# Attention's four PSUM banks: two tiles of two banks instead of one tile with views over any two, and a new order

## The chip, the cores and the metric

The kernel runs on one core of a Trainium2 chip, as one launch. The metric is the time of the launch on the device in microseconds (us); lower is better. A core has five engines, each with an instruction queue of its own that it works through in order: TensorE (PE; its weight loads are shown apart as PEld), VectorE (DVE), ScalarE (ACT), GpSimd (POOL) and SyncE (SP, which here issues the DMAs). Results of TensorE land in PSUM, which has eight banks of 512 fp32 per partition.

## The reference

Chunked attention with eight memory keys in front of each window, and behind it a gated feed-forward (fp32 in and out; the three FFN weights arrive as float64):

```python
# attention: batch 4, 8 heads, 768 steps, head size 64, chunks of 32
k_ctx = k[:, :, max(0, c0 - 16) : min(S, c0 + 32 + 8)]
k_full = concatenate([mem_k, k_ctx]);  v_full = concatenate([mem_v, v_ctx])
scores = scale * q_c @ k_full.T
a = exp(scores - max(scores));  a = a / (sum(a) + 1e-9)
x[:, :, c0 : c0 + 32] = a @ v_full
# FFN: 512 -> 1024 -> 512
h = maximum(x @ w_in, 0)
conv = sum over k of conv_w[k] * shifted h          # 3 taps along the sequence
out = (h * sigmoid(conv)) @ w_out
```

## The kernel before

**Work.** Attention is cut into 32 steps (batch, half of the sequence, pair of heads) and these into 18 groups: groups 0 to 3 hold one step each, groups 4 to 17 two (m is the number of steps). One group is a chain over four engines. On PE the scores (L382, 48 matmul records a step); on DVE the row maximum (L391); then either a subtraction on DVE and one exp on ACT (L396, L400), or six exps a step straight from PSUM on ACT, with the maximum as bias (L416); clearing of the edge; on DVE the row sum and its reciprocal (L433, L437); the normalisation on DVE or POOL (L440); the turning of the result, on PE (the turn, L452, followed by a copy out of PSUM on ACT, L455) or by way of DVE and a DMA (L462 to L477); on PE the product with the values (L496, 48 records a step); and from its result a rounded part on ACT (the high part, L510) and what is left on DVE (the low part, L513). High and low part are what the FFN reads.

The FFN's matmuls are in three passes (high by high, high by low, low by high): ffn_in (L528, 768 matmuls of 384 columns), the relu that empties its PSUM bank (L538), the gate (L549 to L578 on DVE, ACT and POOL) and ffn_out (L590, 600 matmuls, most of 512 columns). The float64 weights are turned into a high and a low fp32 part on ACT, DVE and POOL (L273 to L352), beside the attention of the first three batches.

**PSUM.** Four banks belong to the FFN (four tiles f). The other four are one tile, `banks`; the pool named s hands out bank numbers 0 to 3. Scores and values take two numbers each, a turn one or two (as many as the group has steps), and `view` makes the access: banks a to z in steps of z - a, so 0 and 1, or 0 and 2, or 1 and 3.

**Order.** Every operation is put down with the function that issues it; `Plan.run` then issues them in the order of the table ORDER, 1301 numbers. Nothing is rearranged behind it: on each engine the instructions stand as ORDER has them, and what waits for what across the engines is drawn from the tiles that they read and write. A tile is given its buffer when its first operation in ORDER is issued, and the buffer goes back behind its last. Strings such as TAP, MULT, LO, NORM hold a letter for each group or FFN column block that says which engine does a step.

Of the kernel before, what the change touches and what calls it, by code (L numbers as in the profile page):

```python
# [21 lines left out]
NG = NC // 4  # L22
# [9 lines left out]
W_IN, W_OUT, W_CONV = "CCCCMRmM", "MCMMMCCM", "r"  # L32
TAP = "AAVAAAAAAAAAAAAAAAVAAAVAVVVVAVAV"
MULT = "VVGGGGGVVVVVVGGGGGVGVVVVGVVVVVVG"
LO = "VVVVVGVVVVVVVVVGGGGVGVGGVVGVVVGV"
SOFT = "AAVAVVVCVVCVVAVVVC"
NORM = "GGVGGVGGVVVVGVVGVG"
CLEAR = "GAGGGAGGAVVGGVAGVG"
KEEP = "NKNNNNNNNNNNKNKKKKNNKKKNNKKKNNNN"
# [146 lines left out]
def act(n, psum=False, ptr=0):  # L186
    return ((192 if psum else 238) + n) / 1.2 + 93 * ptr
# [3 lines left out]
def attention_then_gated_ffn(  # L191
# [44 lines left out]
    slots("top", 4, [P, 4 * NG])  # L236
    slots("z", 4, [P, 4 * NG])

    banks = psum.tile([P, 4, 512], F32, name="banks")
    plan.pool("s", list(range(4)))  # L240

    def view(x, n):
# [471 lines left out]
```

## Time and profile before

| | |
|---|---|
| median of 3 runs | 379.67 us (379.25 to 383.1) |
| the profiled execution | 381.81 us, of it 380.0 us span |
| PE busy | 339.1 us (89%) |
| DVE, ACT, POOL busy | 233.8, 190.3, 73.2 us |
| granted TensorE clock, mean | 0.972 of full speed |

The span is the time from the first instruction to the last in the profiled execution; the 1.8 us around it are launch and end. PE has far the most to do, and in the table of stages of 20 us it is busy without a break from 60 to 80, 120 to 140 and, but for 0.92 us, from 200 to 360 us. Rows with [idle before <-releaser] tell how long the engine had stood idle before them, and whose instruction ended the wait; "issue" means that it waited for nothing that the profile shows.

### The profile page before, as it was taken

What the parts mean: (1) busy time and instruction counts of PE and PEld (TensorE: products, weight loads), DVE (VectorE), ACT (ScalarE), POOL (GpSimd) and SP (SyncE); (2) the same over time, 40 slices, a digit from 0 to 9 for tenths busy, and PEclk for the clock granted to TensorE, in tenths of its full rate; (3) what the DMA queues carried; (4) which work ended last, traced back from release to release, by engine and by line L of the source; (5) the groups of instructions that cost most, each with busy time, mean ns of one, the idle gap of its engine ahead of it and who ended that gap; (6) DMA issues with size and microseconds to landing.
All of it is one profiled execution on the core that took longest, in us unless ns stands there. A gap on an engine that the chain in (4) does not pass through costs nothing.

```text
span 380.0 us, 10189 instructions
## 1 busy us (share of the span) xinstructions
PE 339.1 (89%) x4500; PEld 303.1 (80%) x4500; DVE 233.8 (62%) x325; ACT 190.3 (50%) x347; POOL 73.2 (19%) x69
## 2 busy tenths in 40 slices
PE   1378779997988989797999999999999999999996
PEld 0257679996878979796899887789988998888886
DVE  5864767997678978965887968571011558950000
ACT  4624517976583866773546573843243335541011
POOL 0232413023141000251021001511117002121000
PEclk9999989999898998996999999999999999999999
DMA  8992773998350442402321440224000100002022
GB/s 280 403 397 92 285 259 116 298 345 340 103 180 6 139 154 73 117 0 86 116 83 47 155 144 32 101 96 140 2 2 0 55 29 28 2 28 83 29 83 83
DMA packets 24363, 47.60 MB, mean 125 GB/s; under 512 B 2176, under 2 KB 11136, under 8 KB 24320
## 3 DMA queue, kind: packets, MB, share of 16 engines
q1 hardware_dynamic: 24320, 46.96, 35.9%
q8 instruction: 35, 0.57, 0.6%
q14 instruction: 8, 0.07, 0.1%
HBM read 38.30 MB, written 8.65 MB: 124 GB/s over the span
## 4 chain that ended last, share of the span: by engine, by line
PE 82%; DVE 8%; ACT 5%; issue 4%; DMA 1%; DVEq 0%; ACTq 0%
PE f L590 35%; PE f L528 33%; PE banks L496 8%; PE banks L382 5%; ACT e L416 2%; PE banks L452 2%; DVE u L513 1%; DVE e L396 1%; DVE top L391 1%; ACT u L455 1%; DMA w<-in_w_in_dram 1%; ACT u L510 1%; DVE z L433 1%; DVE w_top L283 1%; DVE w L309 1%
## 5 line engine op out<-in xcount | busy, mean ns | idle before, releaser
L528 PE MATMUL f<-u,w_in_hi 128*128 128x384 f32 x512 | 146.1, 352 | 0.0
L590 PE MATMUL f<-w_out_hi,u 128*128 128x512 f32 (+1 forms) x400 | 127.5, 389 | 0.0
L528 PEld LDWEIGHTS f<-u,w_in_hi 128*128 128x128 f32 x512 | 97.5, 196 | 2.2
L528 PE MATMUL f<-u,w_in_lo 128*128 128x384 f32 x256 | 88.8, 347 | 0.0
L590 PEld LDWEIGHTS f<-w_out_hi,u 128*128 128x128 f32 x400 | 74.6, 189 | 15.5
L590 PE MATMUL f<-w_out_lo,u 128*128 128x512 f32 (+1 forms) x200 | 77.5, 388 | 0.0
L558 DVE SCALAR_TENSOR_TENSOR u<-u,cw,u 128x767 f32<-128x767 f32 x64 | 64.3, 1013 | 3.5 <-ACT u L549 2.6
L538 ACT ACTIVATE u<-f 128x384 f32<-128x384 f32 x64 | 31.2, 493 | 47.5 <-PE f L528 43.0
L528 PEld LDWEIGHTS f<-u,w_in_lo 128*128 128x128 f32 x256 | 50.2, 196 | 1.2
L513 DVE TENSOR_TENSOR u<-banks,u 128x768 fp32r<-128x768 f32 (+1 forms) x18 | 15.5, 867 | 49.4 <-ACT u L510 28.5
L590 PEld LDWEIGHTS f<-w_out_lo,u 128*128 128x128 f32 x200 | 37.8, 189 | 7.0
L572 POOL TENSOR_TENSOR u<-u,u 128x768 f32<-128x768 f32 x13 | 25.6, 1973 | 74.6 <-ACT u L571 74.6
L601 ACT COPY w_top<-f 128x512 f32<-128x512 f32 (+1 forms) x25 | 14.2, 568 | 50.7 <-PE f L590 50.6
L496 PEld LDWEIGHTS banks<-u,u 64*64 64x64 f32 x1296 | 25.2, 162 | 10.7 <-ACT u L455 3.4
L496 PE MATMUL banks<-u,u 64*64 64x32 f32 x1296 | 26.9, 242 | 7.3 <-ACT u L455 2.3
L575 ACT CAST u<-u 128x768 fp32r<-128x768 f32 x32 | 26.4, 836 | 13.4 <-DVE u L567 5.5
L562 ACT ACTIVATE u<-u 128x768 f32<-128x768 f32 x32 | 26.5, 844 | 9.9 <-DVE u L558 9.9
L578 POOL TENSOR_TENSOR u<-u,u 128x768 fp32r<-128x768 f32 x10 | 19.0, 1904 | 56.2 <-ACT u L575 35.4
L382 PE MATMUL banks<-k,u 64*32 64x64 f32 x1344 | 17.5, 236 | 9.3 <-issue 7.8
L578 DVE TENSOR_TENSOR u<-u,u 128x768 fp32r<-128x768 f32 x22 | 21.9, 1008 | 6.1 <-ACT u L575 6.1
L510 ACT CAST u<-banks 128x768 fp32r<-128x768 f32 (+1 forms) x18 | 13.1, 733 | 24.5 <-PE banks L496 11.5
L382 PEld LDWEIGHTS banks<-k,u 64*32 64x32 f32 x1344 | 15.0, 110 | 12.8 <-issue 9.4
(57 smaller groups left out, 304.3 us busy)
## 6 DMA issues: line engine op xcount, KB each, us to landing
u<-in_v_dram SPq DMA_DIRECT2D x27, 384.0 KB, 8.3
k<-in_k_dram SPq DMA_DIRECT2D x14, 528.0 KB, 5.8
out_dram<-w_top SPq DMA_DIRECT2D x23, 256.0 KB, 2.1
u<-in_q_dram SPq DMA_DIRECT2D x14, 384.0 KB, 7.8
w<-in_w_in_dram SPq DMA_DIRECT2D x8, 512.0 KB, 6.1
w<-in_w_out_dram SPq DMA_DIRECT2D x8, 512.0 KB, 3.9
t_dram<-w SPq DMA_DIRECT2D x6, 384.0 KB, 4.1
u<-t_dram SPq DMA_DIRECT2D x12, 192.0 KB, 3.3
```

The costliest lines, as they stand in the source:

```text
L382: nc.tensor.matmul(s_of[j * CH : (j + 1) * CH, u, to : to + KW], lhsT=q_[r, c, h], rhs=k_t.t[r, o : o + KW], start=True, stop=True,)
L496: nc.tensor.matmul(a_of[h * D : (h + 1) * D, u, to : to + CH], lhsT=v_c[r, c, h], rhs=a_d.t[r, o : o + CH], start=True, stop=True,)
L510: plan.op("A", act(m * TW, True), lambda: A.copy(out=apart(part[0]()), in_=a_()), (*a,), (hi,))
L513: lambda: V.tensor_tensor(out=apart(part[1]()), in0=a_(), in1=apart(part[0]()).bitcast(F32), op=ALU.subtract),
L528: nc.tensor.matmul(f.t[:, :TW], lhsT=w_in_p[c][:, fc, cc], rhs=x(a), start=(cc == 0 and i == 0), stop=(cc == NCC - 1 and i == 2),)
L538: "A", act(TW, True), lambda: A.activation(h.t[:, hf * TW : (hf + 1) * TW], f.t[:, :TW], AF.Relu, scale=0.5), (f,), ((h, hf),)
L558: lambda j=j, to=to, at=at: V.scalar_tensor_tensor(out=c.t[:, to], in0=h.t[:, at], scalar=w[j], in1=c.t[:, to], op0=ALU.mult, op1=ALU.add) ...
L562: plan.op("A", act(S), lambda: A.activation(c.t, c.t, AF.Tanh), (c,), (c,), table="exp")
L572: plan.op("G", 2.42 * S, lambda: G.tensor_tensor(out=y.t, in0=c.t, in1=h.t, op=ALU.mult), (c, h), (y,), shared=True)
L575: plan.op("A", act(S), lambda: A.copy(out=g_hi.t, in_=y.t), (y,), (g[0],))
L578: lambda: (V if lo == "V" else G).tensor_tensor(out=g_lo.t, in0=y.t, in1=g_hi.t.bitcast(F32), op=ALU.subtract),
L590: nc.tensor.matmul(ps.t[:, :n], lhsT=gs[b, fc][a].t[:, tt * P : (tt + 1) * P], rhs=w_out_p[c][:, fc, o : o + n], start=(fc == 0 and i == 0 ...
```

## The change

The tile `banks` goes. The pool s now holds two PSUM tiles of two banks each, and scores, turns and values each take one of them whole, the one-bank turns of groups 0 to 3 too. From there ORDER was searched anew, and the strings with it: it has 1302 numbers now, since one more of the gate's products goes to POOL, which takes one more ACT instruction (L571). Counted over the strings, 12 instead of 9 of the 32 first taps are on DVE, 18 instead of 19 of the gate's products, 21 instead of 22 of the low parts of g, 8 instead of 9 normalisations. The number of matmuls is the same.

```diff
-TAP = "AAVAAAAAAAAAAAAAAAVAAAVAVVVVAVAV"
-MULT = "VVGGGGGVVVVVVGGGGGVGVVVVGVVVVVVG"
+TAP = "VAVAAAAAAAAAAAAAAAVVAVAVVVVVAVAV"
+MULT = "VVGGGGGVVVVVVVGGVVVVGGVVGVGGVVGG"
...
 ORDER = [
-    326, 13, 12, 337, 29, 28, 60, 45, 327, 332, 44, 333, 61, 328, 348, 335, 15, 329, 330, 359, 16, 338, 343, 14, 17, 339,
+    326, 13, 12, 337, 29, 28, 60, 44, 327, 332, 45, 333, 348, 328, 61, 335, 15, 329, 330, 14, 338, 343, 16, 77, 17, 339, 18,
...
-    banks = psum.tile([P, 4, 512], F32, name="banks")
-    plan.pool("s", list(range(4)))
-
-    def view(x, n):
-        a, z = min(y.t for y in x), max(y.t for y in x)
-        return banks[:, a : z + 1 : max(1, z - a), :n]
-
+    slots("s", 2, [P, 2, 512], pool=psum)
     slots("f", 4, [P, 512], pool=psum)
...
-        s, e, top, z = [Tile("s"), Tile("s")], Tile("e"), Tile("top"), Tile("z")
+        s, e, top, z = Tile("s"), Tile("e"), Tile("top"), Tile("z")
...
-            s_of = view(s, mg * KW)
+            s_of = s.t
...
-        plan.op("PE", 522 * m, scores, (q_d, k_t), (*s,), mode="t32", late=250)
-        s_ = lambda: view(s, mg * KW).rearrange("p u (g k) -> p g u k", k=KW)
+        plan.op("PE", 522 * m, scores, (q_d, k_t), (s,), mode="t32", late=250)
+        s_ = lambda: s.t[:, :, : mg * KW].rearrange("p u (g k) -> p g u k", k=KW)
...
-        a, a_d = [Tile("s"), Tile("s")], Tile("u")
+        a, a_d = Tile("s"), Tile("u")
         if TURN[n] == "P":
-            t = [Tile("s") for _ in range(m)]
+            t = Tile("s")
...
-            plan.op("PE", 245 * m, turn, (e,), (*t,), mode="whole", late=250)
-            plan.op("A", act(m * TW, True), lambda: A.copy(out=steps(a_d.t[:, : m * TW]), in_=view(t, TW)), (*t,), (a_d,))
+            plan.op("PE", 245 * m, turn, (e,), (t,), mode="whole", late=250)
+            plan.op("A", act(m * TW, True), lambda: A.copy(out=steps(a_d.t[:, : m * TW]), in_=t.t[:, :m, :TW]), (t,), (a_d,))
```

On PE, at the start of the program, these are the scores of groups 0 to 3 and the turn and values of group 0. A name in brackets is an engine's counter that the instruction waits for (DVE_49, Activation_49, Pool_49, or a DMA queue's); u_ and k_ are buffers of q and k. Before:

```order
L382 MATMUL banks<-u_115,u_117 32x64 [waits DMAHW2_49,DMAHW1_49]
L382 MATMUL banks<-u_115,u_117 32x64 x23
L382 MATMUL banks<-u_120,u_122 32x64 [waits DMAHW4_49,DMAHW5_49,DVE_49,Activation_49]
L382 MATMUL banks<-u_120,u_122 32x64 x23
L382 MATMUL banks<-u_126,u_130 32x64 [waits DMAHW7_49,DMAHW0_49,DVE_49]
L382 MATMUL banks<-u_126,u_130 32x64 x23
L382 MATMUL banks<-u_133,u_124 32x64 [waits DMAHW1_49,DMAHW6_49,DVE_49,Activation_49]
L382 MATMUL banks<-u_133,u_124 32x64 x23
L452 MATMUL banks<-ident,e_70 128x128 [waits DVE_49,Pool_49]
```

The same place in the changed kernel:

```order
L375 MATMUL s_98<-u_116,u_118 32x64 [waits DMAHW2_49,DMAHW1_49]
L375 MATMUL s_98<-u_116,u_118 32x64 x23
L375 MATMUL s_99<-u_121,u_123 32x64 [waits DMAHW5_49,DMAHW4_49]
L375 MATMUL s_99<-u_121,u_123 32x64 x23
L375 MATMUL s_98<-u_131,u_127 32x64 [waits DMAHW0_49,DMAHW7_49,DVE_49,Activation_49]
L375 MATMUL s_98<-u_131,u_127 32x64 x23
L375 MATMUL s_99<-u_136,u_125 32x64 [waits DMAHW2_49,DMAHW6_49,DVE_49,Activation_49]
L375 MATMUL s_99<-u_136,u_125 32x64 x23
L444 MATMUL s_98<-ident,e_70 128x128 [waits DVE_49,Pool_49]
```

The instructions stand in the same row; the second scores, which write the other two banks, waited for DVE and ACT and now wait for their data alone.

On ACT, behind the turns of groups 12 and 13: u_2391 and u_2456 (u_2396 and u_2457 in the changed kernel) are the copies of the two turns, L510 (L501) the high parts of their values. Before:

```order
L455 COPY u_2391<-banks 128x768 [waits PE_49,Pool_49]
...
L455 COPY u_2456<-banks 128x768 [waits PE_49]
...
L510 CAST u_2515<-banks 128x2x2x192 [waits DMAHW7_49,PE_49]
...
L510 CAST u_2529<-banks 128x2x2x192 [waits DVE_49]
```

And now:

```order
L447 COPY u_2396<-s_99 128x768 [waits PE_49]
...
L447 COPY u_2457<-s_98 128x768 [waits PE_49]
...
L501 CAST u_2516<-s_99 128x2x2x192 [waits PE_49]
...
L501 CAST u_2523<-s_98 128x2x2x192 [waits DVE_49,PE_49]
```

The row of the four is the same; the pair of a group is now on one tile and the other group's on the other.

## Rows read from the trace of the kernel before

**Rows 1.** The page: busy time, share and instructions; PE's fetches (packets, MB, share).

```profile
PE   339.1 (89%) x4500; PEld 303.1 (80%) x4500; DVE 233.8 (62%) x325; ACT 190.3 (50%) x347; POOL 73.2 (19%) x69
q8 instruction: 35, 0.57, 0.6%
```

**Rows 2.** Busy time by stage: length, PE, PEld, DVE, ACT, POOL, clock, DMA share, GB/s.

```profile
0.00:20.00 20.00, 5.46 (x223) 4.18 (x227) 13.44 (x31) 11.25 (x30) 4.61 (x19) 1.00 0.94 345
20.00:40.00 20.00, 15.09 (x356) 12.98 (x349) 11.99 (x24) 7.11 (x14) 5.49 (x6) 1.00 0.68 251
```

**Rows 3.** Timeline of the start: start, length, engine, operation [idle before <-releaser].

```profile
5.79 0.96 PE L382 MATMUL banks<-u,u 64*32 64x64 f32 x48 [5.79 <-DMA u<-in_q_dram]
...
9.57 0.97 PE L382 MATMUL banks<-u,u 64*32 64x64 f32 x48 [2.81 <-ACT e L416]
...
13.64 0.56 DVE L391 TENSOR_REDUCE top<-banks 128x6 f32<-128x384 f32 x1 [1.09 <-ACT e L416]
```

**Rows 4.** The chain that ended last, 23 to 41 us: start, length, what.

```profile
23.57 0.89 PE banks L452 x3
24.49 0.97 DVE top L391
...
25.59 0.89 PE banks L452 x3
...
27.01 0.97 DVE e L396
28.00 0.49 ACT u L455
...
35.73 0.56 PE banks L452 x3
...
38.93 0.84 PE banks L452 x6
```

**Rows 5.** Timeline of PE, waits of attention's matmuls after 100 us.

```profile
108.75 1.60 PE L496 MATMUL banks<-u,u 64*64 64x32 f32 x96 [1.43 <-ACT u L538]
...
172.91 0.85 PE L452 MATMUL banks<-ident,e 128*128 128x128 f32 x6 [1.70 <-DVE e L440]
176.64 2.79 PE L496 MATMUL banks<-u,u 64*64 64x32 f32 x96 [0.90 <-ACT u L455]
...
234.82 0.90 PE L496 MATMUL banks<-u,u 64*64 64x32 f32 x48 [0.92 <-ACT u L455]
```

**Rows 6.** Timeline of all engines at the same places.

```profile
106.70 0.96 DVE L391 TENSOR_REDUCE top<-banks 128x12 f32<-128x768 f32 x1 [3.05 <-ACT e L416]
...
115.77 4.55 PE L496 MATMUL banks<-u,u 64*64 64x32 f32 x192 [1.81 <-DVE u L513]
...
165.94 0.96 DVE L396 TENSOR_TENSOR e<-banks,top 128x768 f32<-128x768 f32 x1 [3.62 <-ACT e L416]
...
175.78 0.80 ACT L455 COPY u<-banks 128x768 f32<-128x768 f32 x1 [4.43 <-PE banks L496]
```

**Rows 7.** Waits of PE: for what, us in total, times, longest.

```profile
PE banks L382 <- issue: 7.8, 4, 2.7
...
PE banks L496 <- issue: 2.1, 1, 2.1
```

**Rows 8.** Timeline of PE at three of those gaps.

```profile
47.20 1.47 PE L382 MATMUL banks<-k,u 64*32 64x64 f32 x128 [0.64 <-issue]
51.04 0.87 PE L382 MATMUL banks<-k,u 64*32 64x64 f32 x63 [2.37 <-issue]
...
155.28 0.32 PE L382 MATMUL banks<-k,u 64*32 64x64 f32 x8 [2.08 <-issue]
```

**Rows 9.** PE in short stretches: length, busy (instructions), granted clock, DMA share, GB/s.

```profile
96.00:100.00 4.00, 4.00 (x34) 0.57 0.62 179
...
156.00:160.00 4.00, 4.00 (x25) 1.00 0.49 139
```

**Rows 10.** The chain that ended last, values of groups 16 and 17.

```profile
269.73 2.93 PE banks L496 x192
```

More of the change, by code (lines that the diff above doesn't have):

```diff
@@ L28 @@
 WC = 512
-W_IN, W_OUT, W_CONV = "CCCCMRmM", "MCMMMCCM", "r"
-TAP = "AAVAAAAAAAAAAAAAAAVAAAVAVVVVAVAV"
-MULT = "VVGGGGGVVVVVVGGGGGVGVVVVGVVVVVVG"
[L35 to L39, printed above, removed]
+W_IN, W_OUT, W_CONV = "CCCCMRMM", "CMCCmMMM", "r"
+TAP = "VAVAAAAAAAAAAAAAAAVVAVAVVVVVAVAV"
+MULT = "VVGGGGGVVVVVVVGGVVVVGGVVGVGGVVGG"
+LO = "VGVVGVVGVVGVVVVVVGVVGVGGVGVGGVVV"
+SOFT = "AAVAVVVCVVCVVCVCVV"
+NORM = "GGVGGVGGVVVVGVVGGG"
+CLEAR = "GAGGVAGGAVVGGVAGVG"
+KEEP = "KNNKKNNNNKNNNNNNNNNKNNNNNNKNNNNN"
 HOME = "wwwwwwwwwwwxwwxxxx"
@@ L385, in scores @@
                             )
-        plan.op("PE", 522 * m, scores, (q_d, k_t), (*s,), mode="t32", late=250)
-        s_ = lambda: view(s, mg * KW).rearrange("p u (g k) -> p g u k", k=KW)
+        plan.op("PE", 522 * m, scores, (q_d, k_t), (s,), mode="t32", late=250)
+        s_ = lambda: s.t[:, :, : mg * KW].rearrange("p u (g k) -> p g u k", k=KW)
         plan.op(
             "V", vec(mw),
-            lambda: V.tensor_reduce(out=each(top), in_=s_(), axis=AX.X, op=ALU.max), (*s,), (top,),
+            lambda: V.tensor_reduce(out=each(top), in_=s_(), axis=AX.X, op=ALU.max), (s,), (top,),
         )
@@ L395, in attention @@
                 "V", vec(mw),
-                lambda: V.tensor_tensor(out=keys(), in0=s_(), in1=wide(top), op=ALU.subtract), (*s, top), (e,),
+                lambda: V.tensor_tensor(out=keys(), in0=s_(), in1=wide(top), op=ALU.subtract), (s, top), (e,),
             )
@@ L416, in less @@
                     A.activation(keys()[:, g // 2, g % 2], s_()[:, g // 2, g % 2], AF.Exp, bias=top.t[:, g : g + 1], scale=SCALE)
-            plan.op("A", 1338 * m, less, (*s, top), (e,), table="exp")
+            plan.op("A", 1338 * m, less, (s, top), (e,), table="exp")
         def edge():
@@ L442, in attention @@
         )
-        a, a_d = [Tile("s"), Tile("s")], Tile("u")
+        a, a_d = Tile("s"), Tile("u")
         if TURN[n] == "P":
-            t = [Tile("s") for _ in range(m)]
+            t = Tile("s")
             def turn():
-                t_of = view(t, NG * P)
                 for g in range(mg):
                     o = g % NG * P
-                    nc.tensor.transpose(out=t_of[:, g // NG, o : o + P], in_=e.t[:, g, 1 : 2 * KW + 1], identity=ident)
-            plan.op("PE", 245 * m, turn, (e,), (*t,), mode="whole", late=250)
-            plan.op("A", act(m * TW, True), lambda: A.copy(out=steps(a_d.t[:, : m * TW]), in_=view(t, TW)), (*t,), (a_d,))
+                    nc.tensor.transpose(out=t.t[:, g // NG, o : o + P], in_=e.t[:, g, 1 : 2 * KW + 1], identity=ident)
+            plan.op("PE", 245 * m, turn, (e,), (t,), mode="whole", late=250)
+            plan.op("A", act(m * TW, True), lambda: A.copy(out=steps(a_d.t[:, : m * TW]), in_=t.t[:, :m, :TW]), (t,), (a_d,))
         else:
@@ L484, in values @@
         def values():
-            a_of = view(a, m * HC * CH)
             for i in range(m):
@@ L496, in values @@
                             nc.tensor.matmul(
-                                a_of[h * D : (h + 1) * D, u, to : to + CH],
+                                a.t[h * D : (h + 1) * D, u, to : to + CH],
                                 lhsT=v_c[r, c, h], rhs=a_d.t[r, o : o + CH], start=True, stop=True,
                             )
-        plan.op("PE", 721 * m, values, (*v_t, (a_d, 0), (a_d, 1)), (*a,), mode="t64", late=250)
-        a_ = lambda: view(a, m * HC * CH).rearrange("p u (s n) -> p u s n", s=m)
+        plan.op("PE", 721 * m, values, (*v_t, (a_d, 0), (a_d, 1)), (a,), mode="t64", late=250)
+        a_ = lambda: a.t[:, :, : m * HC * CH].rearrange("p u (s n) -> p u s n", s=m)
         x_t = [Tile("u", dtype=F32R) for _ in range(m)]
@@ L509, in attention @@
             x_of[b, hf, cc + i] = (lambda c, i=i: part[c]()[:, i * TW : (i + 1) * TW]), hi, lo
-        plan.op("A", act(m * TW, True), lambda: A.copy(out=apart(part[0]()), in_=a_()), (*a,), (hi,))
+        plan.op("A", act(m * TW, True), lambda: A.copy(out=apart(part[0]()), in_=a_()), (a,), (hi,))
         plan.op(
@@ L513, in attention @@
             lambda: V.tensor_tensor(out=apart(part[1]()), in0=a_(), in1=apart(part[0]()).bitcast(F32), op=ALU.subtract),
-            (*a, hi), (lo,),
+            (a, hi), (lo,),
         )
```

111 rows, old and new, of the table ORDER are left out of this document.

## The prediction

> **What bounds the kernel now.** I read the page first: PE is busy 339.1 of 380.0 us, and no other engine comes near it [rows 1]. So the time is PE's work plus PE's idle time, 40.9 us, and a change that leaves the matmuls as they are can only move that idle time and the clock at which PE works. The stages say where it lies: PE is idle 14.54 us from 0 to 20 and 4.91 us from 20 to 40 [rows 2], 19.45 together, of which 5.79 are the first data on their way [rows 3]. Later there are attention's waits [rows 5, 6], and five gaps on "issue", 7.8 + 2.1 = 9.9 us [rows 7]. From 185 us on PE hardly waits.
>
> Then I asked of each wait whether it is a true one. The second scores write banks 2 and 3 and stand idle 2.81 us until ACT has read banks 0 and 1 [rows 3]. The maximum at 13.64 reads banks 0 and 1, and waits 1.09 us for an ACT instruction that reads banks 2 and 3 [rows 3]. So all accesses to `banks`, reads too, run in one file in the order of ORDER, whichever banks they touch. That is what two tiles take away: two files, side by side. The instruction lists of both kernels agree: the second scores lose their wait for DVE and ACT.
>
> **The start, to the values of groups 3 and 4 at 41 us.** What can go at most is the idle time to 40 us without the first data, 19.45 - 5.79 = 13.7 us. From 23.57 to 28.49 the chain is turn, maximum, turn, copy, subtraction, copy: 0.89 + 0.97 + 0.89 + 0.49 + 0.97 + 0.49 us and links, 4.9 us in one file [rows 4]. Maximum and subtraction belong to group 4, turns and copies to groups 2 and 1. In two files turn, copy, turn, copy takes 0.89 + 0.49 + 0.89 + 0.49 and three links of some 0.05, or 2.9 us (the second turn now waits for the first copy, because both use one tile, where they had a bank each; that is in the sum), with the DVE work, 1.94 us, beside it: 2.0 us saved. From 35.73 to 39.77 the same pattern comes once more, for groups 3, 4 and 5: 4.0 us [rows 4], of which DVE's two, about 1.9, go beside: 2.0. From 9.57 to 23.57 the same false waits stand, but DVE there has the conversion of the weights between its attention steps, 13.44 busy us of the first 20 [rows 2], and in the new order conversions still stand ahead of the second maximum; I take 0.5 us. Sum 4.5 us; bounds 2.0 (one of the two stretches) and 13.7.
>
> **88 to 121 us.** Values of group 8 wait 1.43 us until 108.75 [rows 5]. The page names a relu on ACT, but a relu touches none of the four banks; on DVE group 11's maximum, on the other pair of banks, had waited 3.05 us for group 10's exps until 106.70 [rows 6], and its subtraction behind it, as long again, ends at 108.7. Values of group 8 are let in behind that. Both waits are false, and 1.43 us go. Values of groups 10 and 9 wait 1.81 us for the low part of group 8 [rows 6]. In the new kernel group 10 still takes the tile that group 8 leaves, so that wait is true, but what it waits for comes some 2 us sooner; I take all of it. They then run at 4.55 us for 192 records [rows 6], where groups 16 and 17 need 2.93 [rows 10]: 1.6 us of clock to come back. The fetch (below) takes about as much away. Sum 1.43 + 1.81 = 3.2; bounds 1.4 and 4.9.
>
> **165 to 180 us.** The subtraction of group 14 waits 3.62 us for the exps of group 13 [rows 6], false; behind it on DVE, in order, stand conversions, group 13's sum and its normalisation, for which the turn waits 1.70 us until 172.91 [rows 5]. That goes. ACT's copy at 175.78 waits 4.43 us, the last of it for the values of group 12, on the other banks [rows 6]; the values of group 13 wait 0.90 for it [rows 5], and then run at 2.79 us for 96 records where 1.47 is to be had [rows 5, 10]. 1.70 + 0.90 + 1.3, less 1.5 for the fetch: 2.4; bounds 0.9 and 3.9.
>
> **The fetch, which speaks against the change.** At 47.20 PE runs exactly 128 matmul records, with their weight loads 256 instructions, and then waits 2.37 us on "issue"; at 155.28 it is 2.08 [rows 8]. PE's instructions come in 35 packets of together 0.57 MB [rows 1], 16 KB each. Counted in the instruction list, all five gaps lie a multiple of 256 instructions apart. So a block of 128 scores runs for 1.47 us and the next block comes 1.47 + 2.08 = 3.6 to 1.47 + 2.37 = 3.8 us after that block began. A block that runs shorter makes PE wait for the rest. I counted the blocks of both kernels: five of the short blocks of before come again with the same mixture within five matmuls, so 9.9 us of gaps stay. Three more hold 124 to 128 value records, 1.95 us at full speed: in groups 10 and 9, 12 and 13, 14 and 15. Before, false waits and the slow clock stretched these, and nothing was lost. Once they go, a fetch wait of 1.6 to 1.9 us takes their place. This I charged above; for groups 14 and 15 it cancels the 0.92 us of 234.82 [rows 5], so nothing is gained. And one is new: a block that held 110 value records and 17 of the FFN, in groups 16 and 17, now holds 127 value records. That costs 1.6 to 1.9 us, and after most such gaps PE works for a while near the lower of its two levels (1.2 of 2.4 GHz: granted 0.57 on average in the four us behind 96, yet 1.00 behind 156 [rows 9]); (1 - 0.57) x 4 = 1.7 us. I charge 2.5; bounds 0 and 3.6.
>
> The Trainium skill ("Runtime: NRT & Kernel Launch", section Instruction fetch mechanics) has the block of 256 instructions, which this trace shows, but calls the cost of crossing a boundary mostly hidden. By that the last charge would be 0, and the time that of the first rival below; the five gaps speak against it.
>
> **What else moves.** A tap more or less on DVE or ACT, and one product more on POOL with one more ACT instruction, lie beside PE: DVE has 146 idle us, ACT 190, POOL 307 [rows 1]. Behind the last ffn_in stand 273 matmuls of ffn_out in the new list (258 before), which cover what is late there. Uncovered, a product that goes from DVE (0.72 us an instruction on average) to POOL and ACT (1.06 and 0.55) costs 0.9 us. 0, bounds -1 and +1.
>
> Sum: 4.5 + 3.2 + 2.4 + 0 - 2.5 = 7.6 us. The profiled execution took 381.81 us, span 380.0; it would become 374.2. It lies 2.1 us above the median of 379.67, which therefore becomes **372.1 us**.
>
> **Rivals.** *The fetch costs nothing* (blocks come early where PE's clock and the other DMA traffic let them). Then every charge is lifted: 4.5 + (1.43 + 1.81 + 1.6) + (1.70 + 0.90 + 1.3) + 0.92 = 14.2, or 365.5 us. For it: the gap behind 155.28 cost no clock [rows 9]. Against: the five gaps themselves, at four places of the program.
>
> *Something else is last in the same places.* At the start DVE with the conversions, whose in-order queue and not the banks holds attention back; late, true dependences. Only 2.0 at the start and 1.43 and 1.70 remain, less 2.5 and about 2 for waits at new places: 379 us. For it: DVE's 13.44 of the first 20 us.
>
> *Slower.* All four blocks of values pay the gap and the lower clock, 1.75 + 1.7 = 3.5 us each, 13.8 together; and the start gives 2.0 alone. Gains without charges are then 2.0 + 4.8 + 3.9 + 0.9 = 11.6. The kernel is slower as soon as a block costs over 2.9 us; if it costs as much as the longest gap of before, 2.7 + 1.7 = 4.4 [rows 7, 9], it is 17.6 - 11.6 = 6.0 us slower: 385.7.
>
> That the waits stay is excluded by the instruction list; that they are true at other places is the second rival.
>
> **How the numbers follow.** The forecast, 367 to 376 us, gets 0.50; the first rival 0.12; the second 0.20; the third, from no change to 386, 0.12; 0.06 is for half a gain, 376 to 378. The range of 8 in 10 takes in the forecast, nearly all of the first rival and most of the second: 364.5 to 380. One per cent, 3.8 us, is about what a measurement here can tell from no change. Faster by over 1% (under 375.9): 0.50 + 0.12 and a little, 0.64. Within 1%: the second rival, the half gain, half of the third: 0.29. Slower by over 1%: 0.07.
>
> **What would show it.** In the profile of after: the second scores start between 8 and 9 us; the values of groups 3 and 4 near 37 instead of 41 us; no idle time of PE before the values of group 8 and the turn of group 13; in the values of groups 9, 13 and 15 gaps on "issue" instead of waits for ACT and DVE; a new gap in the values of groups 16 and 17; five old gaps as before. The prediction is wrong if PE's idle time to 40 us stays near 19 us, if the blocks of values show no gap, or if PE waits after 185 us, where I expect no change but the one gap.

## Result: 367.9 us, and the profile after

The changed kernel took 367.86 us (median of 4 runs, 367.3 to 368.23), the kernel before 379.89 us beside it (4 runs, 379.25 to 383.1). The ratio is 0.9666, 95% interval 0.961 to 0.9722: 12.0 us less, where the forecast had 7.6. The profiled execution's span went from 380.0 to 366.2 us, 13.8 us less; 1.8 us of these come from which execution was profiled (381.81 us with a median of 379.89 before, 368.02 with 367.86 after).

The page of after: busy times.

```profile
PE 334.5 (91%) x4500; PEld 299.4 (82%) x4500; DVE 236.8 (65%) x325; ACT 187.2 (51%) x346; POOL 82.1 (22%) x71
```

PE's busy time fell by 4.6 us [rows 1], for the same matmuls. The mean granted clock (0.972 and 0.980) accounts for some 380.0 x 0.028 - 366.2 x 0.020 = 3.3 us of it; the rest lies mostly at the start, as told below. PE's idle time fell from 40.9 to 366.2 - 334.5 = 31.7 us. The waits of PE in after show what is left of it (columns: what waited for what, us in total, times, longest):

```profile
PE s L375 <- issue: 10.1, 5, 3.0
PE s L375 <- DMA u<-in_q_dram: 8.3, 2, 5.6
PE s L487 <- issue: 3.8, 4, 1.4
PE s L375 <- ACT e L409: 2.9, 2, 1.9
...
PE f L519 <- issue: 0.7, 1, 0.7
PE s L444 <- issue: 0.5, 1, 0.5
```

The gaps on "issue" are 10.1 + 3.8 + 0.7 + 0.5 = 15.1 us, where they were 9.9 [rows 7]. All other idle time went from 31.0 to 16.6 us. So the span's 13.8 us are 14.4 of waits less, 4.6 of matmuls that ran faster, and 5.2 of fetch gaps more. After 45 us PE waits for DVE or ACT nowhere: [rows 5] have no counterpart.

The timeline of PE in after, at the places that answer to [rows 3, 5, 6, 8] and at the new gaps:

```profile
9.30 0.96 PE L375 MATMUL s<-u,u 64*32 64x64 f32 x48 [2.74 <-DMA u<-in_q_dram]
...
30.46 1.01 PE L375 MATMUL s<-k,u 64*32 64x64 f32 x77 [1.02 <-issue]
...
41.42 1.47 PE L375 MATMUL s<-k,u 64*32 64x64 f32 x127 [2.03 <-issue]
44.98 1.17 PE L375 MATMUL s<-k,u 64*32 64x64 f32 x64 [2.09 <-issue]
...
103.24 0.77 PE L487 MATMUL s<-u,u 64*64 64x32 f32 x37 [0.35 <-issue]
...
112.36 0.44 PE L519 MATMUL f<-u,w_in_hi 128*128 128x384 f32 x1 [0.70 <-issue]
...
145.38 0.34 PE L375 MATMUL s<-k,u 64*32 64x64 f32 x14 [1.89 <-issue]
...
165.80 0.82 PE L487 MATMUL s<-u,u 64*64 64x32 f32 x41 [0.83 <-issue]
...
168.85 2.21 PE L375 MATMUL s<-k,u 64*32 64x64 f32 x192
...
222.59 0.65 PE L487 MATMUL s<-u,w 64*64 64x32 f32 x27 [1.23 <-issue]
```

The chain of after: DVE's last piece at the start, and the values of groups 4 and 3, of groups 10 and 9, and of groups 16 and 17:

```profile
19.80 0.97 DVE e L433
...
35.23 2.23 PE s L487 x144
...
108.01 2.93 PE s L487 x192
...
252.69 2.93 PE s L487 x192
```

Busy time by stretch in after (length, PE, PEld, DVE, ACT, POOL, clock, DMA share, GB/s):

```profile
0.00:20.00 20.00, 7.25 (x322) 5.92 (x325) 13.79 (x33) 11.53 (x32) 5.31 (x19) 1.00 0.92 339
20.00:40.00 20.00, 17.00 (x427) 14.77 (x412) 16.64 (x32) 10.22 (x19) 7.01 (x7) 1.00 0.86 312
...
45.00:51.00 6.00, 6.00 (x79) 5.83 (x79) 3.30 (x6) 2.39 (x5) 0.51 (x2) 0.50 1.04 388
92.00:96.00 4.00, 4.00 (x18) 3.91 (x17) 2.32 (x4) 0.12 (x1) 0.00 (x0) 0.57 0.18 69
...
147.00:150.00 3.00, 3.00 (x11) 3.00 (x10) 2.08 (x4) 2.74 (x4) 2.17 (x2) 0.50 0.51 175
...
166.00:170.00 4.00, 4.00 (x159) 3.27 (x155) 2.97 (x5) 2.83 (x6) 0.00 (x0) 1.00 0.02 4
```

And two stretches and one row of PE's timeline of the kernel before, which the prediction did not have:

```profile
176.00:180.00 4.00, 3.36 (x98) 3.20 (x99) 0.37 (x1) 2.20 (x4) 1.82 (x1) 0.50 0.33 102
180.00:184.00 4.00, 3.50 (x95) 2.64 (x96) 2.78 (x4) 3.49 (x7) 0.00 (x0) 0.82 0.00 0
```

```profile
183.16 2.13 PE L382 MATMUL banks<-k,u 64*32 64x64 f32 x192 [0.51 <-DVE u L513]
```

Busy time up to the values of groups 4 and 3, and from there to the end of the values of groups 10 and 9, in the kernel before and then in after:

```profile
0.00:41.33 41.33, 21.87 (x577) 18.24 (x580) 26.76 (x57) 19.69 (x46) 10.10 (x24) 1.00 0.82 301
41.33:120.32 78.99, 68.75 (x1556) 64.83 (x1555) 61.79 (x90) 47.48 (x96) 19.43 (x19) 0.94 0.65 216
...
0.00:35.23 35.23, 20.10 (x577) 16.96 (x580) 25.75 (x56) 19.17 (x46) 10.13 (x23) 1.00 0.88 324
35.23:110.94 75.71, 68.21 (x1555) 64.61 (x1555) 61.10 (x94) 46.21 (x94) 18.15 (x17) 0.93 0.64 224
```

Where the 13.8 us lie is read from places that come in both kernels. The values of groups 4 and 3 begin at 35.23 instead of 41.33: 6.1. The values of groups 10 and 9 end at 108.01 + 2.93 = 110.94 instead of 115.77 + 4.55 = 120.32 [rows 6], 9.4 earlier, of which the gap at 112.36 takes 0.7 again: 8.7. The scores behind the values of group 13 begin at 168.85 instead of 183.16: 14.3. From there to the end 0.5 us are lost again. Counted in both traces, the same number of matmuls of each shape stands ahead of each of these points, so the differences can be read as they are.

### The profile page after: what moved, and what is told of

The parts are those of the page before. It is cut to its first block, busy times and chain, and to the rows that moved or that the text cites. A ratio compares the mean times of both kernels' runs of the same rounds, so it can differ in the third digit from the quotient of the medians.

```text
span 366.2 us, 10198 instructions
## 1 busy us (share of the span) xinstructions
PE 334.5 (91%) x4500; PEld 299.4 (82%) x4500; DVE 236.8 (65%) x325; ACT 187.2 (51%) x346; POOL 82.1 (22%) x71
## 4 chain that ended last, share of the span: by engine, by line
PE 89%; issue 4%; DVE 3%; DMA 2%; ACT 1%; SPq 0%; ACTq 0%
PE f L519 39%; PE f L581 37%; PE s L487 7%; PE s L375 4%; PE s L444 2%; DMA w<-in_w_in_dram 2%; DVE w L302 0%; DVE z L426 0%; DVE top L384 0%; ACT e L409 0%; DVE w_top L283 0%; SPq L251 0%; DVE w L296 0%; DVE e L433 0%; DVE w L291 0%
## 5 line engine op out<-in xcount | busy, mean ns | idle before, releaser
L519 PE MATMUL f<-u,w_in_hi 128*128 128x384 f32 x512 | 145.5, 351 | 0.7 <-issue 0.7
L519 PEld LDWEIGHTS f<-u,w_in_hi 128*128 128x128 f32 x512 | 97.1, 195 | 3.0 <-issue 1.2
L519 PE MATMUL f<-u,w_in_lo 128*128 128x384 f32 x256 | 88.7, 347 | 0.0
L549 DVE SCALAR_TENSOR_TENSOR u<-u,cw,u 128x767 f32<-128x767 f32 x64 | 67.9, 1075 | 5.4 <-ACT u L540 4.5
L519 PEld LDWEIGHTS f<-u,w_in_lo 128*128 128x128 f32 x256 | 50.1, 196 | 1.1
L563 POOL TENSOR_TENSOR u<-u,u 128x768 f32<-128x768 f32 x14 | 29.4, 2106 | 53.4 <-ACT u L562 42.9
L592 ACT COPY w_top<-f 128x512 f32<-128x512 f32 (+1 forms) x25 | 14.3, 570 | 49.4 <-PE f L581 46.7
L553 ACT ACTIVATE u<-u 128x768 f32<-128x768 f32 x32 | 26.9, 842 | 14.6 <-DVE u L549 14.4
L569 POOL TENSOR_TENSOR u<-u,u 128x768 fp32r<-128x768 f32 x11 | 21.7, 1978 | 51.5 <-issue 25.6
L569 DVE TENSOR_TENSOR u<-u,u 128x768 fp32r<-128x768 f32 x21 | 24.8, 1194 | 12.0 <-ACT u L566 8.8
L504 DVE TENSOR_TENSOR u<-s,u 128x768 fp32r<-128x768 f32 (+1 forms) x18 | 15.4, 862 | 24.9 <-PE f L519 15.0
L375 PE MATMUL s<-k,u 64*32 64x64 f32 x1344 | 17.9, 235 | 11.1 <-issue 10.1
L375 PEld LDWEIGHTS s<-k,u 64*32 64x32 f32 x1344 | 15.2, 110 | 14.5 <-issue 12.3
L487 PEld LDWEIGHTS s<-u,u 64*64 64x64 f32 x1296 | 21.9, 142 | 5.0 <-issue 2.5
L487 PE MATMUL s<-u,u 64*64 64x32 f32 x1296 | 23.6, 226 | 1.9 <-issue 1.2
L558 DVE SCALAR_TENSOR_TENSOR u<-u,u 128x768 f32<-128x768 f32 x18 | 21.4, 1191 | 5.8 <-ACT u L553 5.8
```

The lines of the kernel that those rows point to most:

```text
L375: nc.tensor.matmul(s_of[j * CH : (j + 1) * CH, u, to : to + KW], lhsT=q_[r, c, h], rhs=k_t.t[r, o : o + KW], start=True, stop=True,)
L487: nc.tensor.matmul(a.t[h * D : (h + 1) * D, u, to : to + CH], lhsT=v_c[r, c, h], rhs=a_d.t[r, o : o + CH], start=True, stop=True,)
L504: lambda: V.tensor_tensor(out=apart(part[1]()), in0=a_(), in1=apart(part[0]()).bitcast(F32), op=ALU.subtract),
L519: nc.tensor.matmul(f.t[:, :TW], lhsT=w_in_p[c][:, fc, cc], rhs=x(a), start=(cc == 0 and i == 0), stop=(cc == NCC - 1 and i == 2),)
L549: lambda j=j, to=to, at=at: V.scalar_tensor_tensor(out=c.t[:, to], in0=h.t[:, at], scalar=w[j], in1=c.t[:, to], op0=ALU.mult, op1=ALU.add) ...
L553: plan.op("A", act(S), lambda: A.activation(c.t, c.t, AF.Tanh), (c,), (c,), table="exp")
```

## Experiments

Two theories stood against each other first. *The tile*: one tile is one file of accesses, whatever banks they touch, and it costs the false waits. *The order*: the new ORDER and strings, searched with more numbers to choose from, do it, and the tile is by the way.

**One tile, the new order.** The two buffers of the pool are fixed halves of one tile; all else is after.

```diff
-    slots("s", 2, [P, 2, 512], pool=psum)
+    banks = psum.tile([P, 4, 512], F32, name="banks")
+    plan.pool("s", [banks[:, 0:2], banks[:, 2:4]])
```

> The new order and strings, but the four banks one tile again, with two fixed halves that the groups take in turn. Theory (the gain is that two files of accesses run side by side, and the new order is only good because it can count on that): the false waits come back, PE's idle time to 40 us goes from 15.7 back to 18 or more, the waits before the values of groups 8, 13 and 15 come back, and the kernel takes 378 to 388 us. Rival (the order and the strings made the gain, the tiles little): 367 to 371 us.

Measured: 383.68 us (median of 10 runs, 380.69 to 385.92), ratio 1.0063 [1.0023, 1.0103] to the kernel before, which took 381.6 us beside it (median of 13 runs). The whole gain is gone. PE's timeline of this kernel:

```profile
10.48 0.97 PE L376 MATMUL banks<-u,u 64*32 64x64 f32 x48 [3.75 <-ACT e L410]
...
40.91 0.85 PE L445 MATMUL banks<-ident,e 128*128 128x128 f32 x6 [1.66 <-DVE e L390]
...
110.88 1.87 PE L488 MATMUL banks<-u,u 64*64 64x32 f32 x96 [2.14 <-issue]
...
173.67 0.85 PE L445 MATMUL banks<-ident,e 128*128 128x128 f32 x6 [1.06 <-DVE e L434]
176.97 1.60 PE L488 MATMUL banks<-u,u 64*64 64x32 f32 x96 [0.92 <-ACT u L448]
```

The waits of the second scores [rows 3] and of the turn and the values of group 13 [rows 5] are back with their releasers, and so is that of the values of group 15 (0.92 us at 234.31), even where the order differs. PE's idle time to 40 us is 20.4 us, where 18 or more was expected. One expected wait did not come: the values of group 8 show none for ACT or DVE, but a gap of 2.14 us on "issue". The halves share no bank and no stride, so it isn't the strided view over "any two banks" that orders the accesses, but the tile.

**Two tiles, the old order.** Before's ORDER and strings with two tiles. In that order an operation can come when both tiles are in use; it is then put off until one is free, with all that depends on it. On PE one turn moves by this.

```diff
-        for i in ORDER:
+        held = []
+        def ready(i):
+            _, after, tiles = self.ops[i]
+            need = defaultdict(int)
+            for x in tiles:
+                need[x.pool] += x.slot is None
+            return after <= done and all(len(idle[p]) >= n for p, n in need.items() if n)
...
+        for i in issued():
```

> The two tiles with the order and the strings of before; an operation that finds no free tile is put off until one is, which moves one turn at the start and nothing else. Theory: most of the 12 us come from the tiles, so 368 to 373 us, with the waits before the values of groups 8 and 13 and before the turn of group 13 gone. Rival (the search made the gain): 376 to 381 us.

Measured: 369.85 us (369.23 to 370.74, 4 runs), ratio 0.97 [0.9648, 0.9753], span 367.6. Its PE timeline at the places of [rows 5]:

```profile
113.18 0.44 PE L537 MATMUL f<-u,w_in_hi 128*128 128x384 f32 x1 [0.77 <-issue]
...
167.69 0.79 PE L505 MATMUL s<-u,u 64*64 64x32 f32 x41 [1.30 <-issue]
```

No wait stands ahead of the values of group 8 or the turn of group 13; behind them lie the same fetch gaps as in after. So the tiles alone bring 11.8 us, 3.0%, against the 381.6 us of the kernel before beside them, and both changes together 3.3%; what the new order and the strings add, the intervals of the two ratios don't tell from none. The theory of the order falls.

**Where the fetch borders lie.** The prediction charged the fetch by place, so the next kernels move the borders and nothing else: N small matmuls ahead of the first scores, into FFN banks whose content is overwritten before it is read. Each is an fp32 product of four instructions, so 27 move all borders by 108 and 64 by 256, that is by nothing.

```diff
+    for _ in range(27):
+        nc.tensor.matmul(plan.pools["f"][3][:32, :64], lhsT=ident[:64, :32], rhs=ident[:64, :64], start=True, stop=True)
```

> The new kernel with 27 small matmuls, 108 instructions, ahead of the first scores, where PE waits for data anyway; what they write is overwritten. They move every border of a block of 256 instructions. Theory (a block that runs shorter than some 3.3 us makes PE wait for the rest): counted at the durations of the trace, the sum of the gaps on issue after the start falls from 9.4 to 5.0 us, and with the clock that comes back 4 to 8 us are gained: 360 to 364 us. Rival (the gaps come from what the DMA engines are doing, or from the kind of matmul, not from the borders): 367 to 369 us, gaps at the same matmuls as before.

Measured: 362.99 us (360.71 to 363.22), ratio 0.9505 [0.9449, 0.9562]. PE's timeline:

```profile
1.36 5.86 PE L241 MATMUL f<-ident 64*32 64x64 f32 x53 [1.36 <-POOL ident masks.py:199]
...
31.99 0.42 PE L377 MATMUL s<-k,u 64*32 64x64 f32 x3 [2.59 <-issue]
40.90 0.89 PE L489 MATMUL s<-u,u 64*64 64x32 f32 x44 [1.77 <-issue]
...
81.94 0.44 PE L489 MATMUL s<-u,u 64*64 64x32 f32 x8 [4.13 <-issue]
```

Every gap stands at another matmul, though nothing but the count ahead of it changed: they belong to the borders and not to an operation. The time came out as the theory said, its count did not: the gaps from 60 us on sum up to 4.13 + 0.90 + 2.02 = 7.1 us, against 9.5 in after, where 5.0 had been counted.

> The same with 64 small matmuls, 256 instructions, so that the borders fall where they were. Theory: gaps at the same matmuls and 367 to 369 us; that tells the shift from what the small matmuls do otherwise (to the clock at the start, above all). Rival (the small matmuls themselves help): the same time as with 108 instructions.

Measured: 375.54 us (374.81 to 376.0), ratio 0.9846 [0.9794, 0.9899]. As a control of the time it failed, by its own making:

```profile
1.35 13.75 PE L241 MATMUL f<-ident 64*32 64x64 f32 x127 [1.35 <-POOL ident masks.py:199]
```

All into one part of the array, the small matmuls took 13.75 us and put the start off. As a control of the places it holds: the gaps stand at the matmuls of after (in front of x127, x64, x55, x42, x14, x41 and x27, 1.0 to 3.1 us).

**Quick ones.** So that the added matmuls cost little, they now take turns over four column parts and two row halves. N is 22, 56, 64, 45 and 27 in the kernels below.

```diff
+    for i in range(N):
+        j, u = i // 2 % 4, i % 2
+        r = ident[u * D : (u + 1) * D]
+        nc.tensor.matmul(plan.pools["f"][2 + u][j * CH : (j + 1) * CH, :KW], lhsT=r[:, :CH], rhs=r[:, :KW], start=True, stop=True)
```

> The new kernel with 22 small matmuls, 88 instructions, ahead of the first scores; they take turns over the parts of the array as scores do, so that they end long before the data are there. Theory (borders of blocks): counted with 4.9 us to the next block while loads run (to 100 us) and 3.1 later, a lead of 8 instructions and 0.8 us of slow clock behind a gap, the cost of the gaps falls from 19.3 to 12.8 us: 361 to 364 us, with at most six gaps over 0.3 us behind 40 us, and none in the values of groups 10 and 9, 14 and 15. Rival (the slow small matmuls of shift108 did something else): 367 to 369.

Measured (22 of them): 364.27 us (362.69 to 365.1), ratio 0.9533 [0.9494, 0.9571], a little over the 361 to 364 that was expected. Behind 40 us it has four gaps; one of them, 1.03 us, stands in the values of groups 10 and 9, where none was expected.

> The same with 56, 224 instructions. Theory: the borders fall worse than in the changed kernel, 23.5 us instead of 19.3: 369 to 374 us. Above all the block in the values of groups 16 and 17, whose border stood exactly ahead of the first of these matmuls and which showed no gap, now begins 16 matmuls inside; a gap of about 1.0 us comes there if the fetch had only had a lead from the slow FFN matmuls ahead of the border. Rival (the fetch is quick there for another reason, such as idle DMA engines): no gap in these values.

Measured (56): 366.47 us (363.72 to 370.71), ratio 0.9571 [0.9513, 0.9629], which is better than expected. The profiled execution took 370.71 us, so only places are read from it. A gap of 1.07 us stands in the values of groups 14 and 15, now ahead of their last 11 matmuls. In groups 16 and 17 there is none, where the expectation had about 1 us from a border 16 matmuls into them. That step of it fell, and what the rival had said came; quick180 (N = 45) speaks against the rival, and the DMA windows further down show what was early.

> The control again, 64 small matmuls, 256 instructions, now quick ones: theory, the gaps stand at the same matmuls as in the changed kernel and the time is 367 to 369 us, since nothing is late at the start. If it is over 370 or under 366, the small matmuls themselves change something.

Measured (64, the control): 368.93 us (367.26 to 369.56), ratio 0.9645 [0.9606, 0.9684]: as after. The quick matmuls alone bring nothing.

> After with 45 of the quick small matmuls, a shift by 180 instructions. It brings a border exactly ahead of the first value matmul of groups 14 and 15, where after has a border 38 matmuls into them and a gap of 1.23 us, and it moves the border of groups 16 and 17 from their first matmul to 38 matmuls in. Sequencer theory (a block is asked for when PE's sequencer crosses the border before it, and behind slow FFN matmuls the sequencer is 1.5 us or more ahead of the array): no gap in groups 14 and 15, the packet for them starting over 1 us before their first value matmul; in groups 16 and 17 a gap between 0 and 0.9 us. Rival (the gap belongs to the place, as DMA or semaphores there have it): 1.0 to 1.3 us again in groups 14 and 15, none in 16 and 17. Time 364 to 369 us by both.

Measured (45): 366.76 us (363.13 to 368.36), ratio 0.9627 [0.9571, 0.9683]. Counted again, the border is not exactly ahead of the first value matmul of groups 14 and 15, as the expectation says, but 52 matmuls ahead of it, in ffn_out, and the next 76 matmuls in. There the gap is gone. In groups 16 and 17, where after has none, it has come:

```profile
250.20 0.65 PE L491 MATMUL s<-u,w 64*64 64x32 f32 x27 [0.94 <-issue]
```

It stands ahead of the last 27, as after's stands at 222.59 in groups 14 and 15. The rival, that a gap belongs to the place, falls, and so does that of the kernel with N = 56, since there too the DMA engines moved nothing between the two packets at 247.7 and 251.3, shown further down. 0.94 is a little more than the 0 to 0.9 that was expected.

> After with 27 of the quick small matmuls ahead of the first scores, so the same shift of the borders by 108 instructions as the 27 slow ones of shift108 made, but without their 5.9 us of one array part. Borders theory: gaps on issue at the same matmuls as in shift108 and again about 12 us together, three or four of them from 40 us on; the first scores still wait for their data until 5.6 to 5.8 us. Time 361 to 364 us. Rival (the slow matmuls themselves helped, for instance by covering the wait for data, and not where the borders lie): 365 to 368 us, as after and the shift by 88.

Measured (27): 362.12 us (360.78 to 365.82), ratio 0.9532 [0.9464, 0.96], span 360.9. The borders' theory holds: the slow matmuls of shift108 did not make its time, and the first scores still waited for their data, if until 6.38 instead of 5.6 to 5.8 us. From 40 us on there are six gaps instead of three or four, two of them of 0.3 us or less. Both kernels with this shift beat before and after. Its gaps on "issue" are 12.4 us at least where after has 15.1, and its mean granted clock 0.986 instead of 0.980, which is 366.2 x 0.020 - 360.9 x 0.014 = 2.3 us by that estimate; together 5.0 of the span's 5.3. This sum doesn't order the other shifts, whose runs lie up to 7 us apart. By the ratios, the shifts by 88 and 108 are worth 1.4 to 1.7% against after; the intervals of those by 180 and 224 overlap with that of after. What a shift is worth can't be foretold closer from the count of gaps.

## Why the prediction was right, and where its sum was off

**The mechanism holds.** That the tile orders its accesses, and that this is what the waits rest on, is shown by one_tile_new_order and two_tiles_old_order. After lies between the forecast and the first rival, in which the fetch costs nothing; that rival's reason is not met, as there are 15.1 us of gaps.

**The start: 6.1 instead of 4.5.** Ahead of the turn of group 1 (23.57 us before, 21.39 after) waits of 2.20 us went, where the sum had 0.5. From there to 28.5 us 1.30 went instead of 2.0, and from 33.5 to 39 us 0.76 + 1.60 = 2.36 instead of 2.0. Two further terms are not in the sum. Up to the values of groups 4 and 3 PE was busy 20.10 instead of 21.87 us for the same matmuls, 1.77 less. And two new fetch gaps, 0.52 at 23.74 and 1.02 at 30.46, took 1.54 away: 2.20 + 1.30 + 2.36 + 1.77 - 1.54 = 6.1. The faster matmuls show in pairs of ffn_in, before (L528) and in after (L519):

```profile
32.06 0.84 PE L528 MATMUL f<-u,w_in_hi 128*128 128x384 f32 x2
...
28.25 0.51 PE L519 MATMUL f<-u,w_in_hi 128*128 128x384 f32 x2
```

The rows of stretches give a clock of 1.00 for both places, but the trace of before holds no record of the clock ahead of 34.7 us. A lower clock until then would fit the pace; it is not shown. The second scores did lose their wait for ACT, but waited 2.74 us for their own data instead and began at 9.30, not between 8 and 9: there the gain was 0.3. The chain of after goes through DVE until 19.80 + 0.97 = 20.8 us, as the second rival had it for this stretch: of the 13.7 us that could go at most, 12.75 + 3.00 - 5.60 = 10.2 are still idle.

**88 to 121: 2.6 instead of 3.2.** Both waits went and the values run at 2.93 us for 192 records, as reckoned. That the sum came out so close is in part luck. From the values of groups 4 and 3 on, 4.55 us of waits went, since 0.99 at 46.32 and 0.32 at 90.59 went too, which the sum did not have. But the three old gaps between take 2.03 + 2.09 + 3.03 = 7.15 us instead of 5.70, and the new ones 0.35 + 0.70 instead of the 1.6 that I set against the clock. And PE's busy time fell by 68.75 - 68.21 = 0.54 us alone: the values gained 1.6, and elsewhere, as from 45 to 51 us, the clock is low for longer. So 4.55 + 0.54 - 1.45 - 1.05 = 2.6.

**121 to 185: 5.6 instead of 2.4.** Here lies the largest error of the gains. The waits of 1.70 and 0.90 went, and the gap behind them was 0.83, not 1.5. What was mis-sized is the clock: I gave back 1.3 us on the values of group 13 alone, while before has the clock at 0.50 from 176 to 180 and at 0.82 from 180 to 184, so up to 4 x 0.50 + 4 x 0.18 = 2.7 us, the ffn_out behind the values included; after has 1.00 from 166 to 170. The wait of 0.51 us at 183.16 went as well, and I had not seen it. With the two old gaps at 134 and 145, which are 0.8 us shorter than the same two of before (1.44 + 1.89 against 2.09 + 2.08), this is 1.70 + 0.90 - 0.83 + 2.7 + 0.51 + 0.8 = 5.8.

**The fetch: the gaps came, the largest charge did not.** In the values of group 13 and of group 15 the waits for ACT and DVE turned into gaps on "issue", 0.83 and 1.23 us, as said; for the values of groups 10 and 9 the gap lies just behind them. The five old gaps came again with 2.03 + 2.09 + 3.03 + 1.44 + 1.89 = 10.5 us, where 9.9 had stood. But the values of groups 16 and 17 run without a gap, where I charged 2.5. And behind the gaps of the values the clock stayed at 1.00, as the stretch from 166 on shows; it fell to 0.50 and 0.57 behind those of 45, 90 and 145 us alone. The step that failed is "a block that runs shorter makes PE wait for the rest": it takes it that the next block is asked for when the array begins the one before it. The windows of after with the DMA's traffic show when it is asked for, since between 218.8 and 223.8 us nothing else moves; 164 GB/s over 0.1 us are one packet of 16 KB.

```profile
218.80:219.80 1.00, 1.00 (x74) 1.00 (x76) 1.00 (x2) 0.97 (x2) 0.00 (x0) 1.00 0.00 0
219.80:219.90 0.10, 0.10 (x20) 0.10 (x16) 0.10 (x1) 0.10 (x1) 0.00 (x0) 1.00 0.83 164
...
221.30:222.50 1.20, 0.06 (x4) 0.00 (x0) 1.20 (x3) 0.37 (x1) 0.00 (x0) 1.00 0.00 0
...
223.65:223.75 0.10, 0.10 (x3) 0.06 (x2) 0.10 (x1) 0.00 (x0) 0.00 (x0) 1.00 0.71 164
```

The packet starts at 219.8, PE goes on at 222.59, 2.7 to 2.8 us later, and the next packet starts 1.1 us after that. In quick180 the packet of its gap at 250.20 starts at 247.70, 2.5 us ahead, and the next one again 1.1 us behind:

```profile
247.70:247.75 0.05, 0.05 (x17) 0.05 (x13) 0.00 (x0) 0.00 (x0) 0.00 (x0) 1.00 1.34 328
...
251.30:251.35 0.05, 0.05 (x2) 0.05 (x1) 0.00 (x0) 0.00 (x0) 0.00 (x0) 1.00 1.52 328
```

So a block takes 1.1 + 2.5 to 2.8 = 3.6 to 3.9 us from the crossing of a border, as the prediction had it, if PE's sequencer (which works through the queue and hands the matmuls to the array) and the array cross together, which they do behind a gap. In the values of groups 16 and 17 they don't. The DMA queues of after from 250.95 to 251.10 us have this row:

```profile
q8 instruction: 1, 0.02, 38.9%
```

and from 252.6 to 254.5 no packet at all. By the count the block that begins with the first value matmul, at 252.62, has its successor asked for some 1.6 us before: the array still had the matmuls of ffn_in to do, while the sequencer had gone on past the border. In quick224, where the border lies 16 matmuls into the values that begin at 255.22, the packet is early as well:

```profile
254.15:254.25 0.10, 0.10 (x2) 0.10 (x1) 0.00 (x0) 0.00 (x0) 0.00 (x0) 1.00 0.68 164
```

A border on which the sequencer comes while FFN matmuls are queued is paid for by them; a border deep in a run of small matmuls is not. In after it is 38 matmuls into the values of groups 14 and 15, and there it costs 1.23 us; in quick180 it is 38 into those of 16 and 17, and costs 0.94. That the queue of matmuls is what lets the sequencer run ahead fits these four places and was not tested by itself.

The Trainium skill ("Runtime: NRT & Kernel Launch", section Instruction fetch mechanics) calls the crossing mostly hidden. The trace agrees where FFN matmuls are queued, with no gap from 223 us to the end in after, and differs inside runs of scores and values, with 10.1 + 3.8 = 13.9 of the 15.1 us of gaps.

**The rest: -0.5 instead of -2.5.** 234.82's 0.92 became 1.23, as the prediction's "nothing is gained" had it within 0.3, and nothing waits after 223 us. Shifts of tap, normalisation and products show nowhere on PE's path.

Counted up, 6.1 + 2.6 + 5.6 - 0.5 = 13.8 us, against 4.5 + 3.2 + 2.4 - 2.5 = 7.6 (both of spans): the charge in groups 16 and 17 (2.0), the clock and the wait of 176 to 184 us (1.9 of 3.2) and the start (1.6: matmuls that ran faster, and waits before 23 us) make most of the difference.

## What to carry to other kernels

Where buffers are used by engines side by side, give each a tile of its own: views into one tile cost some 12 us of 380 here, by waits between accesses to different banks and by what hung on them. Look for such waits in rows whose releaser works on other data than the waiter. When waits go, expect the work that had been stretched to show what was under it, here the instruction fetch; its borders can be moved with some tens of harmless instructions, worth up to 1.7% here, and the profile of one shifted kernel says more than a count.

## What the runs showed of the hardware that was not expected

Small matmuls of one shape took 5.86 us for 53 records, 0.11 us each, when all went to one part of the array; taking turns over eight parts they took

```profile
1.36 1.10 PE L243 MATMUL f<-ident 64*32 64x64 f32 x54 [1.36 <-POOL ident masks.py:199]
```

in quick108, 0.02 us each. And the fetch can come later where the DMA engines are busy with loads: the packet for the gap that ends at 41.42 in after starts between 39.0 and 39.2 us; the block before it, by the count, began with the values at 35.6, 3.5 us earlier and not 1.1, and in between the DMA engines are full:

```profile
35.50:39.00 3.50, 3.50 (x145) 3.36 (x137) 3.41 (x7) 2.31 (x5) 1.18 (x2) 1.00 0.95 329
```

So, as I read it, at the start a block can come 5.8 us after the one before, and a gap there is as much the loads' doing as the border's.
